# Linear-attention sums kv with the features as the loaded operand, in 32 by 32 outputs, without a transpose

## The chip, the core and the metric

The kernel runs on one core of a Trainium2 chip. The metric is the device time of one execution in microseconds (us). A core has five engines with instruction lists of their own: TensorE (PE in the profile; its weight loads are shown apart, as PEld), VectorE (DVE), ScalarE (ACT), GpSimd (POOL) and SyncE (SP, here the main DMA queue). TensorE multiplies a loaded operand (the stationary one, held in the 128x128 array) by a streamed one (the moving one) and writes to PSUM, which has banks of 128 partitions by 512 f32 values.

## The reference

Two branches read the same x (2048 rows, 512 columns) and are mixed by a gate. The change is in the first branch.

```python
# A: linear attention, 32 heads of 16
q, k, v = x @ wqkv                                    # split by head
pq = einsum("bhsd,hdf->bhsf", q, w_phi); pk = einsum("bhsd,hdf->bhsf", k, w_phi)
phi_q = concatenate([softmax(pq), softmax(-pq)])      # 32 features for each head
phi_k = concatenate([softmax(pk), softmax(-pk)])
kv  = einsum("bhsf,bhsd->bhfd", phi_k, v)             # sums over all 2048 rows: 32 x 16 for each head
z   = phi_k.sum(over s)
num = einsum("bhqf,bhfd->bhqd", phi_q, kv)
o   = num / (einsum("bhqf,bhf->bhq", phi_q, z) + 1e-6)
a   = o @ wo
# B: dense 512 -> 1376, Mish, 1376 -> 512
b   = mish(x @ w1 + b1) @ w2
g   = sigmoid(x . gate_w)
out = g * a + (1 - g) * b
```

## The kernel before

The kernel has two stages. Stage A goes over x in 8 chunks of 256 rows (two tiles of 128). It makes the features of k (a tile E of 128 rows by 1024 columns: two softmaxes of 512) and the values v (128 x 512), adds E up into zacc on POOL, adds E times v up in PSUM (kv), and stores the projected q to DRAM. Stage B goes over 4 blocks of 512 rows: the dense branch by 11 column tiles (up, then mi, hi, lo on ACT and POOL, then dn), the features of q, the product with kv (nu), the output projection (wo), and the mix. Large products are made of f32 split into a high and a low part in the rounded f32r type, three products for each; kv, num and the fused weights (fuse) are plain f32 products.

The order on every engine is written out by hand. Strings such as FIRST, EVEN, ODD, NEXT, LAST (stage A) and BLOCK0, BLOCK1, BLOCK (stage B) list steps by name; a word with a quote mark belongs to the chunk before, one with a plus to the next. The wrapper `pin` keeps each engine's instructions in the order in which they were written, and all matmuls go through the helper `mm` (line 101), all ACT work through `act` (line 121). So an engine that waits holds up everything behind it in its own list.

The steps that the change touches:

- `kv` (line 322) is run as `kv' kv` at the end of chunks 1, 3 and 5 (ODD), so for two chunks at once, and once for each of the chunks 6 and 7, in LAST. All sums go to one PSUM bank of the tag "kv", 256 of its 512 columns. For each of a chunk's two tiles it goes over u = 0..7 and r = 0, 1. One product loads 32 columns of v (two heads of 16) and streams 64 columns of E (the same two heads, both softmaxes, a = 0, 1). The output has 32 partitions (v) and 64 columns (features). Its start partition, 0, 32, 64 or 96, goes round with u and r.
- `km` (line 449, DVE) multiplies the sums by `mask`, which keeps the blocks in which feature and value belong to the same head, and writes them twice, spread over 512 columns.
- `kt_` (line 455, in BLOCK0 between up3 and mi3) turns this by four TensorE transposes of 128x128 against the identity `ident`, into a PSUM bank of the tag "a" (a ring of three that up, half of num, half of wo and the projections share), and ACT copies it to `kvb` (features in the partitions).
- `nu` (line 593) loads 64x32 pieces of kvb and streams the features of q, 256 columns, in all four blocks.
- `ident` and `mask` are made on POOL at the start (lines 188 to 192).

Of the kernel before, what the change touches and what calls it, by code (L numbers as in the profile page):

```python
# [8 lines left out]

F32 = mybir.dt.float32  # L10
# [5 lines left out]
P = 128  # L16
# [5 lines left out]
NG = 4  # L22
SC = 256
NCH = S // SC
# [36 lines left out]

BLOCK0 = """
    up0 mi0 hi0 lo0 gr lq3 S1 rS1 mx2 mn2 d02 d12 up1 @z mi1 hi1 lo1 T0 D0 m0 de0 rd0 sc0 es0 tr0 up2 mi2 hi2 lo2 dn0
    T1 D1 m1 de1 rd1 sc1 es1 tr1 mv0 lq0+ lq1+ mx3 mn3 d03 d13 up3 @kt mi3 hi3 lo3 dn1
    up4 mi4 hi4 lo4 WL0 dn2 E2 S2 T2 rS2 D2 m2 de2 rd2 sc2 es2 tr2 up5 mi5 hi5 lo5 WL1 dn3 E3 ge gg up6 mi6 hi6 lo6 dn4
    up7 mi7 hi7 lo7 dn5 nu0 oh0 S3 T3 rS3 ol0 D3 m3 de3 rd3 sc3 es3 tr3 mv1 up8 mi8 hi8 lo8 dn6
    mx0+ mn0+ d00+ d10+ mx1+ mn1+ d01+ d11+ lq2+ lq3+ wo0 ag0 wo1 ag1 E0+ E1+ S0+ T0+ rS0+ D0+ m0+ de0+ rd0+ sc0+ es0+ tr0+
# [22 lines left out]
def tile_gated_mix(ctx: ExitStack, tc: tile.TileContext, xT, wv, wkT, wqT, bd, w1a, w1b, b1, w2a, w2b, wo, out):  # L90
    nc = tc.nc
    const = ctx.enter_context(tc.tile_pool(name="const", bufs=1))
# [4 lines left out]
    pin = tc.keep_in_program_order  # L97
    V, G_, A_, Sy = nc.vector, nc.gpsimd, nc.scalar, nc.sync

    def mm(*a, **k):  # L100
        return pin(nc.tensor.matmul(*a, **k))  # L101

    def T(shape, dt, tag, bufs, name):
        nm[0] += 1
        return sp.tile(shape, dt, name=f"{name}_{nm[0]}", tag=tag, bufs=bufs)
# [7 lines left out]
    def k2(name, tag, dt=F32):  # L113
        return T([P, 512], dt, tag, {"pq": 3, "io": 4, "hl": 8}[tag], name)

    def psum(name, tag, bufs={"a": 3, "dn": 4, "kv": 1}):
        nm[0] += 1
        return pp.tile([P, 512], F32, name=f"{name}_{nm[0]}", tag=tag, bufs=bufs[tag])

    def act(out_, in_, fn=AF.Copy, **k):  # L120
        return pin(A_.activation(out_, in_, fn, **k))  # L121
# [60 lines left out]
    md = k2("md", "io")[:, :P].rearrange("p (h f) -> p h f", f=DH)  # L182
# [2 lines left out]
    pin(G_.affine_select(md, md, pattern=[[DH, 8], [0, DH]], compare_op=ALU.is_ge, fill=0.0, base=DH - 1, channel_multiplier=-1))  # L185
    b1s = const.tile([P, NF], F32, name="b1s")
    pin(G_.dma_start(b1s, b1))
    ident = const.tile([P, P], F32, name="ident")
    make_identity(nc, ident)
    mask = const.tile([P, 2, 2, 32], F32, name="mask")  # L190
    for a in range(2):
        pin(G_.tensor_add(mask[:, :, a, :], *[md[:, o : o + 4, :].rearrange("p (r h) f -> p r (h f)", r=2) for o in (0, 4)]))
    g_sb = const.tile([P, S // P], F32, name="g_sb")
    og_sb = const.tile([P, S // P], F32, name="og_sb")
    ge_sb = const.tile([P, S // P], F32, name="ge_sb")
    kvb = const.tile([P, NG, P], F32, name="kvb")


    steps = {}
# [1 line left out]
    def at(key, name, fn):  # L201
        steps.setdefault((key, name), []).append(fn)
# [11 lines left out]
    kvs = []  # L214
# [69 lines left out]
    def a_ops(c):  # L284
        key = ("A", c)
        P_ = psA[c] = {}
        for t in range(2):
            d = {}
            Es[c, t] = d

            def k_(t=t):
                P_["k", t] = proj(xs[c], t, wkh, wkl, "a")

            def v_(t=t):
                P_["v", t] = proj(xs[c], t, wvh, wvl, "dn" if c or t else "kv")

            def q_(t=t):
                P_["q", t] = proj(xs[c], t, wqh, wql, "a")

            def ve(t=t):  # L300
                vs[c, t] = k2("v", "io")
                act(vs[c, t], P_["v", t])

            def qe(t=t):
                P_["qs", t] = k2("qs", "pq")
                act(P_["qs", t], P_["q", t])

            def st(t=t):
                i = 2 * c + t
                pin(Sy.dma_start(pqd[i * P : (i + 1) * P, :], P_["qs", t]))  # L310

            at(key, f"k{t}", k_)
            at(key, f"v{t}", v_)
            at(key, f"q{t}", q_)
            at(key, f"ve{t}", ve)
            at(key, f"qe{t}", qe)
            at(key, f"st{t}", st)
            feat_ops(key, t, lambda t=t: P_["k", t][:, :], d)
            at(key, f"ml{t}", lambda d=d: scale_by(d, V))
            at(key, f"z{t}", lambda d=d: pin(G_.tensor_add(zacc, zacc, d["E"])))  # L320

        def kv():
            if not kvs:
                kvs.append(psum("kvp", "kv")[:, : NG * 64].rearrange("p (g f) -> p g f", g=NG))
            (kvp,) = kvs
            for t in range(2):
                E, v = Es[c, t]["E"], vs[c, t]
                Ev = E[:, :].rearrange("p (a r b x) -> p b r a x", a=2, r=2, b=8)
                for u in range(8):
                    for r in range(2):  # L330
                        o = (u % 2) * 64 + 32 * r
                        mm(kvp[o : o + 32, u // 2, :], v[:, u * 64 + 32 * r : u * 64 + 32 * r + 32], Ev[:, u, r, :, :],
                           start=(c == 0 and t == 0 and u < 2), stop=(c == NCH - 1 and t == 1), skip_group_check=True)

        at(key, "kv", kv)
        if c + 1 < NCH:
            def xh():
                new_x(c + 1)
                for j in range(2):
                    x_hi(c + 1, j)  # L340

            at(key, "xh", xh)
            for j in range(2):
                at(key, "xl", lambda j=j: x_lo(c + 1, j, G_))
        if c + 2 < NCH:
            at(key, "ldx", lambda: ldx(c + 2))
# [91 lines left out]
    B = {}  # L438

    def mid_ops():  # L440
        key = ("A", NCH - 1)

        def zh():
            B["zs"] = [k4("zs", "tx", F32R) for _ in range(2)]
            act(B["zs"][0], zacc)

        def km():
            B["km"] = k2("km", "io")
            shape = [P, NG, 2, 64]
            m = mask[:, :, :, :].rearrange("p r a f -> p r (a f)")[:, None, :, :].to_broadcast(shape)  # L450
            pin(V.tensor_mul(B["km"][:, :].rearrange("p (g r f) -> p g r f", g=NG, r=2), kvs[0][:, :, None, :].to_broadcast(shape), m))

        def kt_():
            pt = psum("kvT", "a")
            for G in range(NG):
                pin(nc.tensor.transpose(pt[:, G * P : (G + 1) * P], B["km"][:, G * P : (G + 1) * P], ident))  # L456
            act(kvb, pt[:, :].rearrange("p (g d) -> p g d", g=NG))

        def z():
            B["zb"] = k4("zb", "z")  # L460
            for a in range(2):
                ps = psum("z", "dn")
                for j in range(2):
                    mm(ps, onr, B["zs"][j][:, a * 512 : (a + 1) * 512], start=(j == 0), stop=(j == 1))
                act(B["zb"][:, a * 512 : (a + 1) * 512], ps)

        at(key, "zh", zh)
        at(key, "zl", lambda: pin(V.tensor_sub(B["zs"][1], zacc, f32(B["zs"][0]))))
        at(key, "km", km)
        at(("B", 0), "@kt", kt_)  # L470
        at(("B", 0), "@z", z)


    def b_ops(b):
        key = ("B", b)
        U, dn, tts, eTs, num, ohl, io = {}, {}, {}, {}, {}, {}, {}
# [66 lines left out]
        for t in range(4):  # L543
            d = {}
# [40 lines left out]
        for h in range(2):  # L585
            def mv(h=h):
                eTs[h] = k8("eT", "eT", F32)[:, :].rearrange("p (t q x) -> p t q x", t=2, q=4)
                for q in range(4):
                    for k in range(4):
                        o = 64 * (k % 2) + 32 * (k // 2)  # L590
                        pin(Sy.dma_start(eTs[h][o : o + 32, :, q, :], tts[h][32 * q : 32 * q + 32, :, k, :]))

            def nu(h=h):
                ev = eTs[h][:, :, :, :].rearrange("p t q (b c) -> p b (t q) c", c=32)
                po = [psum("num", tag) for tag in ("kv", "a")]
                for bh in range(2):
                    for c in range(4):
                        u = 4 * bh + c
                        for r in range(2):
                            o = (u % 2) * 64 + 32 * r  # L600
                            mm(po[r][32 * c : 32 * c + 32, bh * SC : (bh + 1) * SC], kvb[64 * r : 64 * r + 64, u // 2, o : o + 32], ev[64 * r : 64 * r + 64, u, :, :], start=True, stop=True, skip_group_check=True)
                for r in range(2):
                    num[h, r] = po[r]

            def oh(h=h):
                for gp in range(2):
                    ohl[h, gp] = k4("ohl", "oh", F32R)
                    act(ohl[h, gp][:, :512], num[h, gp])

            def ol(h=h):  # L610
                for gp in range(2):
                    pin(V.tensor_sub(ohl[h, gp][:, 512:], num[h, gp], f32(ohl[h, gp][:, :512])))  # L612

            at(key, f"mv{h}", mv)
            at(key, f"nu{h}", nu)
            at(key, f"oh{h}", oh)
            at(key, f"ol{h}", ol)
# [97 lines left out]
    for j in range(2):  # L715
        h, l = [w[:, 2 * j : 2 * j + 2, :].rearrange("p k f -> p (k f)") for w in (wvh, wvl)]
# [93 lines left out]
```

## Time and profile before

| what | value |
|---|---|
| median of 3 runs | 451.06 us (450.77 to 451.5) |
| profiled execution | 451.0 us, its span 449.3 us |
| granted TensorE clock, mean | 0.999 |
| PE busy | 443.9 us (99% of the span) |
| DVE, ACT, POOL busy | 306.0, 195.0, 163.0 us |
| TensorE time of kvp, by the chain | 1.7% of the span |

The profile shows one execution. The span runs from the first to the last instruction; the execution's own time is 1.7 us longer. The groups name a line, an engine, an operation and the tiles out<-in; for matmuls the line is that of the helper, 101, so they are told apart by tiles: kvp are the sums, kvT the transposes, num the product with kv. A matmul record lasts from its start to the modelled end of its passage through the array, so records overlap, and the sum of durations is more than the time taken. The chain of work that ended last is given in pieces: start, length, engine and group, number of instructions.

### The profile page before, as it was taken

Reading aid. Unit: us, or ns where it says so; the run is one execution under the profiler, and the core shown is the slowest. Engines: PE = TensorE matmul, PEld = TensorE weight load, DVE = VectorE, ACT = ScalarE, POOL = GpSimd, SP = SyncE. Lnnn points to the kernel's source line nnn. Section 1 sums busy time; section 2 is a strip of 40 time slices with the busy share of each in tenths; the row PEclk is TensorE's granted clock in tenths of the full one; section 3 lists DMA queues with packets and bytes.
Section 4 is the critical chain, followed back from the end, with each engine's and each line's share of the span. In section 5 each row is a group of like instructions: output and inputs, shape, how many; then the busy total and the mean of one; then the engine's idle time right before and its main releaser. Section 6 shows DMA issues by size and latency. Waiting matters only on the chain.

```text
span 449.3 us, 7222 instructions
## 1 busy us (share of the span) xinstructions
PE 443.9 (99%) x2886; PEld 362.8 (81%) x2886; DVE 306.0 (68%) x408; ACT 195.0 (43%) x269; POOL 163.0 (36%) x102
## 2 busy tenths in 40 slices
PE   8999999999999999999999999999999999999997
PEld 7888888888888888878787887887887888787885
DVE  2798558459399999997979976476967529611003
ACT  3644533444325555627355453534253543244221
POOL 3448687677862345621122212014212122221211
PEclk9999999999999999999999999999999999999999
DMA  7721522514523111405143151331151302030002
GB/s 272 268 95 47 190 69 95 190 15 172 189 84 106 48 24 25 117 19 154 64 125 111 39 148 48 82 107 47 36 149 47 86 13 95 1 82 13 1 0 95
DMA packets 25883, 40.09 MB, mean 89 GB/s; under 512 B 5749, under 2 KB 14197, under 8 KB 25849
## 3 DMA queue, kind: packets, MB, share of 16 engines
q1 hardware_dynamic: 25528, 39.22, 28.6%
q8 instruction: 23, 0.38, 0.3%
q10 hardware_dynamic: 288, 0.39, 0.3%
q14 instruction: 12, 0.09, 0.1%
q0 software_dynamic: 32, 0.01, 0.0%
HBM read 22.82 MB, written 8.40 MB: 69 GB/s over the span
## 4 chain that ended last, share of the span: by engine, by line
PE 98%; DMA 1%; ACT 0%; DVE 0%; issue 0%
PE proj L101 29%; PE up L101 27%; PE down L101 26%; PE wo L101 10%; PE num L101 2%; PE kvp L101 2%; DMA bds<-in_bd_dram 1%; PE fuse L101 1%; PE rest L101 0%; PE z L101 0%; ACT wkh L121 0%; PE warm L101 0%; DVE io L653 0%; PE kvT L456 0%
## 5 line engine op out<-in xcount | busy, mean ns | idle before, releaser
L500 POOL TENSOR_TENSOR l<-act,h 128x512 fp32r<-128x512 f32 x44 | 63.2, 1438 | 221.9 <-ACT h L121 183.6
L121 ACT ACTIVATE act<-up,b1s 128x512 f32<-128x512 f32 x44 | 30.3, 688 | 89.0 <-PE up L101 88.8
L320 POOL TENSOR_TENSOR zacc<-zacc,E 128x1024 f32<-128x1024 f32 x16 | 39.7, 2483 | 42.7 <-DVE E L282 32.6
L121 ACT ACTIVATE E<-E 128x1024 f32<-128x1024 f32 x32 | 33.6, 1059 | 47.3 <-DVE E L267 44.3
L282 DVE TENSOR_TENSOR E<-E,Sm 128x1024 f32<-128x1024 f32 x32 | 45.7, 1427 | 1.1
L271 DVE TENSOR_REDUCE Sm<-E 128x64 f32<-128x1024 f32 x32 | 38.7, 1210 | 5.0 <-ACT E L121 5.0
L101 PE MATMUL wo<-woh,ohl 128*128 128x512 f32 x128 | 40.7, 389 | 0.0
L101 PE MATMUL down<-w2ah,h 128*128 128x512 f32 x96 | 37.5, 390 | 0.0
L101 PE MATMUL down<-w2al,h 128*128 128x512 f32 x96 | 37.4, 390 | 0.0
L101 PE MATMUL down<-w2ah,l 128*128 128x512 f32 x96 | 37.4, 389 | 0.0
L258 DVE TENSOR_REDUCE mx<-proj 128x32 f32<-128x512 f32 x16 | 11.0, 690 | 30.7 <-PE proj L101 30.7
L101 PE MATMUL down<-w2bh,h 128*128 128x512 f32 x78 | 30.5, 391 | 0.0
L101 PE MATMUL down<-w2bl,h 128*128 128x512 f32 x78 | 30.4, 390 | 0.0
L101 PE MATMUL down<-w2bh,l 128*128 128x512 f32 x78 | 30.4, 389 | 0.0
L121 ACT ACT_TABLE_LOAD x19 | 24.4, 1283 | 10.1 <-PE up L101 9.8
L121 ACT ACTIVATE h<-act 128x512 fp32r<-128x512 f32 x44 | 27.8, 632 | 1.4
L612 DVE TENSOR_TENSOR ohl<-num,ohl 128x512 fp32r<-128x512 f32 x16 | 10.3, 683 | 26.5 <-ACT ohl L121 26.3
L101 PEld LDWEIGHTS wo<-woh,ohl 128*128 128x128 f32 x128 | 24.0, 188 | 5.0
L101 PE MATMUL up<-xbh,w1ah 128*128 128x512 f32 x96 | 26.2, 395 | 0.0
L101 PE MATMUL up<-xbh,w1al 128*128 128x512 f32 x96 | 25.7, 390 | 0.0
L101 PE MATMUL up<-xbl,w1ah 128*128 128x512 f32 x96 | 25.7, 390 | 0.0
L405 DVE TENSOR_TENSOR xbl<-xraw,xbh 128x1024 fp32r<-128x1024 f32 x8 | 12.2, 1562 | 19.8 <-ACT xbh L121 19.8
(121 smaller groups left out, 966.6 us busy)
## 6 DMA issues: line engine op xcount, KB each, us to landing
eT<-tt SPq DMA_DIRECT2D x128, 64.0 KB, 2.0
xraw<-in_xT_dram SPq DMA_DIRECT2D x15, 512.0 KB, 4.4
pqd<-qs SPq DMA_DIRECT2D x16, 256.0 KB, 3.1
pq<-pqd SPq DMA_DIRECT2D x16, 256.0 KB, 2.9
out_dram<-io SPq DMA_DIRECT2D x15, 256.0 KB, 2.1
raw<-in_w1a_dram SPq DMA_DIRECT2D x3, 512.0 KB, 4.3
raw<-in_w2a_dram SPq DMA_DIRECT2D x3, 512.0 KB, 4.0
wT<-in_wkT_dram SPq DMA_DIRECT2D x4, 256.0 KB, 5.2
```

Source lines behind the costliest of these rows:

```text
L101: return pin(nc.tensor.matmul(*a, **k))
L121: return pin(A_.activation(out_, in_, fn, **k))
L258: pin(V.tensor_reduce(d[name], hv(src()), axis=AX.X, op=op))
L271: pin(V.tensor_reduce(d["S"], hv(d["E"][:, :]), axis=AX.X, op=ALU.add))
L282: pin(eng.tensor_mul(hv(d["E"][:, :]), hv(d["E"][:, :]), d["S"][:, :, None].to_broadcast([P, 2 * H, DH])))
L320: at(key, f"z{t}", lambda d=d: pin(G_.tensor_add(zacc, zacc, d["E"])))
L405: pin(V.tensor_sub(xb[b][1][:, :, sl], kt(raw[h], SC), f32(xb[b][0][:, :, sl])))
L500: pin(G_.tensor_sub(U[i]["l"], U[i]["a"], f32(U[i]["h"])))
L612: pin(V.tensor_sub(ohl[h, gp][:, 512:], num[h, gp], f32(ohl[h, gp][:, :512])))
```

## The change

The operands of the sums change places: 32 columns of E (two heads, one softmax) are loaded and 32 columns of v are streamed, so there are two products, for a = 0 and 1, where there was one. The output has features in the partitions (start partition 64r + 32a) and values in the columns, which is the layout that `nu` loads. So the transposes, their PSUM bank, the copy to kvb and the identity go. `km` writes kvb directly, 256 columns in place of 512. The mask becomes 128x32, made by three dependent adds. `nu` reads kvb[:, u, :], in pieces of the same shape as before.

```diff
-    T1 D1 m1 de1 rd1 sc1 es1 tr1 mv0 lq0+ lq1+ mx3 mn3 d03 d13 up3 @kt mi3 hi3 lo3 dn1
+    T1 D1 m1 de1 rd1 sc1 es1 tr1 mv0 lq0+ lq1+ mx3 mn3 d03 d13 up3 mi3 hi3 lo3 dn1
...
-    ident = const.tile([P, P], F32, name="ident")
-    make_identity(nc, ident)
-    mask = const.tile([P, 2, 2, 32], F32, name="mask")
-    for a in range(2):
-        pin(G_.tensor_add(mask[:, :, a, :], *[md[:, o : o + 4, :].rearrange("p (r h) f -> p r (h f)", r=2) for o in (0, 4)]))
+    mask = const.tile([P, 32], F32, name="mask")
+    for o in (2, 4, 6):
+        pin(G_.tensor_add(mask, md[:, :2, :].rearrange("p h f -> p (h f)") if o == 2 else mask, md[:, o : o + 2, :].rearrange("p h f -> p (h f)")))
...
-    kvb = const.tile([P, NG, P], F32, name="kvb")
+    kvb = const.tile([P, 8, 32], F32, name="kvb")
...
-                kvs.append(psum("kvp", "kv")[:, : NG * 64].rearrange("p (g f) -> p g f", g=NG))
+                kvs.append(psum("kvp", "kv")[:, :256].rearrange("p (u d) -> p u d", u=8))
...
                 Ev = E[:, :].rearrange("p (a r b x) -> p b r a x", a=2, r=2, b=8)
                 for u in range(8):
                     for r in range(2):
-                        o = (u % 2) * 64 + 32 * r
-                        mm(kvp[o : o + 32, u // 2, :], v[:, u * 64 + 32 * r : u * 64 + 32 * r + 32], Ev[:, u, r, :, :],
-                           start=(c == 0 and t == 0 and u < 2), stop=(c == NCH - 1 and t == 1), skip_group_check=True)
+                        for a in range(2):
+                            o = 64 * r + 32 * a
+                            mm(kvp[o : o + 32, u, :], Ev[:, u, r, a, :], v[:, u * 64 + 32 * r : u * 64 + 32 * r + 32],
+                               start=(c == 0 and t == 0 and u == 0), stop=(c == NCH - 1 and t == 1), skip_group_check=True)
...
         def km():
-            B["km"] = k2("km", "io")
-            shape = [P, NG, 2, 64]
-            m = mask[:, :, :, :].rearrange("p r a f -> p r (a f)")[:, None, :, :].to_broadcast(shape)
-            pin(V.tensor_mul(B["km"][:, :].rearrange("p (g r f) -> p g r f", g=NG, r=2), kvs[0][:, :, None, :].to_broadcast(shape), m))
-
-        def kt_():
-            pt = psum("kvT", "a")
-            for G in range(NG):
-                pin(nc.tensor.transpose(pt[:, G * P : (G + 1) * P], B["km"][:, G * P : (G + 1) * P], ident))
-            act(kvb, pt[:, :].rearrange("p (g d) -> p g d", g=NG))
+            pin(V.tensor_mul(kvb, kvs[0], mask[:, None, :].to_broadcast([P, 8, 32])))
...
-        at(("B", 0), "@kt", kt_)
...
-                            o = (u % 2) * 64 + 32 * r
-                            mm(po[r][...], kvb[64 * r : 64 * r + 64, u // 2, o : o + 32], ev[64 * r : 64 * r + 64, u, :, :], start=True, stop=True, skip_group_check=True)
+                            mm(po[r][...], kvb[64 * r : 64 * r + 64, u, :], ev[64 * r : 64 * r + 64, u, :, :], start=True, stop=True, skip_group_check=True)
```

## The prediction

> **What bounds the kernel now.** I read the page first (engine shares, granted clock, chain by line), then the chain of waits in order of time, then the answers by tile for everything that the diff touches.
>
> ```profile
> PE 443.9 (99%) x2886; PEld 362.8 (81%) x2886; DVE 306.0 (68%) x408; ACT 195.0 (43%) x269; POOL 163.0 (36%) x102
> ...
> PEclk9999999999999999999999999999999999999999
> ...
> PE 98%; DMA 1%; ACT 0%; DVE 0%; issue 0%
> ```
>
> TensorE is the bound from the first product to the last, at full clock. It hardly waits for anybody, so only two things can move the time: the length of its own list of work, and a new wait on that list. Work taken from other engines is worth nothing here. In the chain by time:
>
> ```profile
> 15.36 2.02 PE fuse L101 x128
> ...
> 44.81 1.92 PE kvp L101 x128
> ...
> 138.29 1.03 PE kvp L101 x64
> ...
> 166.19 0.44 PE kvT L456 x4
> ```
>
> The sums of kv stand on the chain five times: three double runs of 1.92 us (44.8, 79.6, 114.4) and two single ones of 1.03 us (138.3, 150.4), 7.82 us together. The transposes stand on it once with 0.44 us. That is all of the chain that the diff edits; the product with kv (num) keeps its shapes.
>
> ```profile
> L101 PEld LDWEIGHTS kvp<-E,v x512: 106/110/111, 44.7 to 151.2; 128*32 128x32 f32 x171
> L101 PE MATMUL kvp<-E,v x512: 218/219/244, 44.7 to 151.2; 128*32 128x64 f32 x171
> L451 DVE TENSOR_TENSOR km<-kvp,mask x1: 627/627/627, 157.1 to 157.1; 128x512 f32<-128x512 f32 x1
> ```
>
> The code issues 8 chunks x 2 tiles x 16 = 256 products and the trace has 512 matmuls, so an f32 product is two instructions with a weight load each. Below, a pair is one load and one matmul.
>
> **How long a pair takes, and why.** A matmul record is 219 ns long, but a double run has 128 in 1.92 us, 15.0 ns each: several are in flight. The start times in the trace say how. In a run four matmuls start 6.7 ns apart (four outputs at partitions 0, 32, 64, 96), then nothing, and 56.0 ns after the first comes the next four. A double run is 32 such groups, 32 x 0.056 = 1.79 us, plus 0.13 us of turning from and to other work; a single one is 16 x 0.056 + 0.13 = 1.03. What are the 56 ns? The four transposes stream 128 columns each over the whole array and start 108 ns apart, the last warm-up products (128 f32 columns) 112 ns apart, some 0.83 ns a column; 64 columns are 53.3 ns. So one strip of the array is busy for 53.3 ns with its 64 columns, four strips work side by side, and 2.7 ns are overhead: the stage is bound by streaming, not by the number of instructions, as far as this trace goes.
>
> **The change part by part.**
>
> *kv sums.* 512 products, so 1024 pairs; each streams 32 columns of v in place of 64 of E, and loads 32 columns as before. The order of the outputs is again 0, 32, 64, 96, so four strips still work side by side. If streaming remains the bound, a group of four takes 32 x 0.83 = 26.7 ns plus overhead, and there are 256 groups in place of 128. For the overhead the trace has two rows. In kvp it is 2.7 ns, but there the load (32 columns) is half as long as the stream (64). After the change both are 32. The fuse stage has that ratio, 64 loaded and 64 streamed:
>
> ```profile
> L101 PEld LDWEIGHTS fuse<-bds,wT x256: 129/135/136, 6.0 to 17.1; 64*64 64x64 f32 x128
> L101 PE MATMUL fuse<-bds,wT x256: 218/218/268, 6.0 to 17.2; 64*64 64x64 f32 x128
> ```
>
> Loads of 32, 64 and 128 columns last 110, 135 and 188 ns (kvp, fuse, z), so loading costs 0.8 ns a column too, and a strip can't be ahead with its loads when they are as long as its stream. There the groups of four come 58.5 ns apart, 5.2 ns over the stream; it shows in the chain (128 matmuls in 2.02 us against 1.92). I take 26.7 + 5.2 = 31.9 ns, because the ratio is that of fuse: 256 x 0.0319 + 5 x 0.13 = 8.82 us, which is 1.00 us more than 7.82. With the overhead of kvp (29.4 ns) it is 8.18, 0.36 more. The other end: if a pair keeps its 15.0 ns however short its stream, 1024 pairs cost twice 7.82, 7.8 us more. A gain I exclude here: the columns streamed per strip are the same and the groups are twice as many. The row nearest to the new shape is fuse, so +1.00 stands in the sum.
>
> Four pairs at 6.7 ns are 26.7 ns, just under 31.9. That is the tight spot: the trace shows this rate only inside a group, never kept up over more than eight.
>
> The Trainium skill speaks against the change at this spot: TensorEngine Tiling, section Instruction Overhead, gives each matmul some 60 cycles, says a free dimension of 1 takes as long as one of 60, and advises not to tile a dimension that is already small. By that rule 32 columns would gain nothing over 64 and the sums would cost 7.8 us more; no stream in this trace is short enough to try it. The Trainium skill's page TensorE: Matmul & The Clock Gate (section Wait — 56ns, not 53.3ns?) has a floor of about 25 ns from start to start, which the trace's 15.0 ns a matmul contradicts across strips; along one strip no run here shows it.
>
> *Transposes.* Four matmuls and the turn to them go. From the start of the product before (165.80) to that of the second product after (166.70) pass 0.90 us, of which two ordinary steps of 0.227 are 0.45; 0.45 us go from the chain, in agreement with the 0.44 above.
>
> *Off the path.* ACT loses the eviction kvb<-kvT (0.60 us at 166.7). km on DVE writes 128x256 in place of 128x512: 0.63 becomes about 0.42 by the 128x256 row wkl<-fuse (0.41 to 0.43). It is still followed by the same reductions, and kvb is ready near 157.5, 33 us ahead of num at 191.1. TensorE waits for neither engine here, so 0. The bank that kvT took between up3 and up4 in the ring of three is now up4's; each user still gets the bank of three users before, so no new wait. POOL loses ident's memset and select (0.20 and 0.29) and has three dependent adds of 128x32 for two of 128x64 (0.33 each); its set-up ends at 4.3 us and its next work starts at 14.8, so 10 us cover that. No DMA is moved.
>
> *Inputs.* E becomes the loaded operand, v the streamed one. DVE has finished E before the runs begin (43.2 for 44.8, 77.9 for 79.6, 112.7 for 114.4, 147.4 for 150.4), so which operand is needed first costs 0.
>
> *Sum*, against the profiled execution, 451.0 us (span 449.3, 1.7 around it; the median of the runs, 451.06, is the same): +1.00 - 0.45 = +0.55, that is 451.6 us. With the small overhead -0.1.
>
> **Rivals.**
>
> *The number of pairs becomes the bound (slower).* TensorE can't take pairs faster than some rate above 8.0 ns (31.9 / 4), the point from which this decides. For it: no stretch of the trace sustains more than a pair in 14 ns. Against it: 6.7 ns inside groups of four and of eight (num). At 10 ns a pair the sums cost 1024 x 0.010 + 0.65 = 10.9 us, +3.1, and 453.6 us in all; at the 15.0 ns of today, 458.4 us. I give 0.35, one third of it to the full price, 458.4. The Trainium skill's rule in TensorEngine Tiling, cited above, would mean that full price.
>
> *Instruction blocks arrive late (slower).* TensorE's program comes in blocks:
>
> ```profile
> q8 instruction: 23, 0.38, 0.3%
> ```
>
> 0.38 MB for the page's 2 x 2886 = 5772 instructions are about 66 bytes each, and 0.38 MB / 23 is 16.5 KB, so some 250 to a block. A double run now uses up one block in 1.9 us and would use two. In the trace the third run (79.6 to 81.5) is followed by blocks at 83.4 and 87.0 only, some 1 us each. If few are held in store, each of the three double runs would stop for 1 to 2 us: 3 to 6 us on top of 451.6, 454.6 to 457.6 us. Against it: the 24 warm-up, 256 fuse and 48 projection pairs up to 17.4 us are 656 instructions, 2.6 blocks, one of them delivered by then, and nothing stalls, so at least two were in store. I give 0.1. The Trainium skill, in Runtime: NRT & Kernel Launch, section Instruction fetch mechanics, gives TensorE 128 KiB in one sentence and two lines of 16 KiB in another; by the first no stop comes, and no run here decides it.
>
> *A real gain.* The chain holds only 0.45 us to remove, so over 0.9 us needs something beyond it, a strip that streams 32 columns in less than half of 53.3 ns (20 ns a group of four would give 256 x 0.020 + 0.65 = 5.8 us, and 448.5 in all). Against it: 0.83 ns a column in every f32 row. 0.05.
>
> **Numbers.** The stream-bound forecast has 0.5, by itself 450.8 to 452.0. A measurement of this kernel tells 0.2% (0.9 us) from no change, so 450.2 to 452.0 is the same. Of the forecast 0.44 lie there, 0.05 above (an overhead of 7 ns would do), 0.01 below. Slower: 0.05 + 0.35 + 0.1 = 0.50; faster: 0.05 + 0.01 = 0.06. The range goes from 450.6 to 456.5: it leaves out the gain (0.06), the full price of the pair-bound rival (0.12) and the end of the late blocks (0.02), and takes in the rest.
>
> **What would show it.** In the changed profile: 1024 matmuls 128x32 in kvp, double runs of 256 at about 2.17 us, single ones of 128 at 1.15, no kvT, no new idle time of PE. A double run near 3.8 us proves the pair-bound rival. Pauses at one place within a run, different from run to run, with a block landing at their end, prove the blocks. If the kvp runs are as forecast and the time is not, the step that failed is the one that calls all else covered.

## The result, and the profile after

The changed kernel takes 463.03 us (median of 6 runs, 461.06 to 464.9), against 451.1 for the kernel before: ratio 1.0264, with a 95% interval of 1.0251 to 1.0277. The forecast of 451.6 us and the whole range (450.6 to 456.5) are missed. The profiled execution is the quickest of the six, 461.06 us with a span of 459.2 (449.3 before). Its page:

```profile
PE 447.8 (98%) x3394; PEld 365.9 (80%) x3394; DVE 305.6 (67%) x408; ACT 194.6 (42%) x268; POOL 162.9 (35%) x101
...
PEclk9999999899999999999999999999999999999999
...
q8 instruction: 26, 0.43, 0.4%
...
PE 97%; issue 2%; ACT 0%; DVE 0%
```

TensorE is still the bound, with 508 pairs more (512 for the sums, less 4 transposes). New are 2% "issue" in the chain, time in which the engine waited for nothing that the profile shows, and one slice with a lower clock. The chain in order of time (start, length, group) has the place:

```profile
44.50 1.79 PE kvp L100 x124
46.29 1.60 issue
47.89 0.92 PE kvp L100 x61
...
81.67 1.56 PE kvp L100 x113
83.23 5.01 issue
88.25 1.51 PE kvp L100 x95
89.75 33.51 PE proj L100 x144
123.26 2.46 PE kvp L100 x179
125.72 3.40 PE proj L100 x14
129.12 0.17 issue
```

TensorE stops in the middle of the first double run for 1.60 us, in the second for 5.01 us, and 3.4 us behind the third for 0.17 us; the third run itself goes through in 2.46 us. The two single runs follow at 148.19 and 160.56 with 1.25 and 1.30 us. (The numbers of instructions in this view leave some out: the timeline has 256 pairs in a double run, 179 of them ahead of the first stop and 161 ahead of the second.)

Where the 9.9 us of span went, by this chain: stops 1.60 + 5.01 + 0.17 = 6.78; the runs of sums without the stops 10.79 in place of 7.82, 2.97 more; the projections behind the second stop 33.51 in place of 32.86, and those behind the third run 3.40 + 18.90 in place of 21.98, together 0.97 more; from the first up product to the end 297.34 in place of 297.84, 0.50 less; the start 0.31 less. Sum 9.91. This is the quickest of the six executions. The spans of the others are 0.4 to 4.0 us longer, at mean clocks of 0.988 to 0.993 against 0.996 here, so the loss of clock that is described below is probably larger in them; their stops were not traced.

### The profile page after: what moved, and what is told of

It reads as the page before. It is cut to its first block, busy times and chain, and to the rows that moved or that the text cites. A ratio compares the mean times of both kernels' runs of the same rounds, so it can differ in the third digit from the quotient of the medians.

```text
span 459.2 us, 8235 instructions
## 1 busy us (share of the span) xinstructions
PE 447.8 (98%) x3394; PEld 365.9 (80%) x3394; DVE 305.6 (67%) x408; ACT 194.6 (42%) x268; POOL 162.9 (35%) x101
## 4 chain that ended last, share of the span: by engine, by line
PE 97%; issue 2%; ACT 0%; DVE 0%
PE proj L100 29%; PE up L100 26%; PE down L100 26%; PE wo L100 9%; PE kvp L100 2%; PE num L100 2%; PE warm L100 1%; PE fuse L100 1%; PE rest L100 0%; PE z L100 0%; ACT wkh L120 0%; DVE io L640 0%; DVE ones L169 0%
## 5 line engine op out<-in xcount | busy, mean ns | idle before, releaser
L279 DVE TENSOR_TENSOR E<-E,Sm 128x1024 f32<-128x1024 f32 x32 | 44.7, 1395 | 1.1
```

Source lines behind the costliest of these rows:

```text
L279: pin(eng.tensor_mul(hv(d["E"][:, :]), hv(d["E"][:, :]), d["S"][:, :, None].to_broadcast([P, 2 * H, DH])))
```

## The experiments

The theory after this result: TensorE's instructions come in blocks of 256, and a block is only fetched when an earlier one has been used up. A double run of 512 short instructions reaches the end of the block in hand before the next has come. I call it the block theory. The rivals: the pairs of the new shape are slow as such, E as the loaded operand is slow, or a run of some length fills something up.

**The runs apart.** In ODD, the sums of the chunk before are moved ahead, so that every run has 128 pairs:

```diff
-    k0 xh mx0 mn0 ...
+    k0 kv' xh mx0 mn0 ...
-    ... q1 qe1 st1 kv' kv
+    ... q1 qe1 st1 kv
```

> The changed kernel, with the sums of the chunk before moved from the end of the odd chunks to behind their first projection (k0): every run of sums has 128 pairs, with some 13 us of projections between two runs. Block theory (TensorE's next block of 256 instructions is asked for only when the one before it begins, and takes 3 to 6 us from then until it can run; a double run uses two blocks in 2.1 us): a run now needs one boundary at most, so the stops of 1.6 and 5.0 us fall under 0.5 us each; 8 runs of 1.25 to 1.30 us, 10.2 us in place of 7.8, less 0.45: 453.0 us. Rival, the pairs themselves are slow (each pair of this shape costs what it costs, stops included): the sums still cost 17 us or more and the time stays at 461 to 465 us.

Measured: 454.03 us, ratio 1.0065 (1.005 to 1.008). The chain has no stop in any run:

```profile
31.40 1.29 PE kvp L100 x99
...
46.56 1.40 PE kvp L100 x98
```

The other six are 1.25 to 1.29 us. So the same pairs, with the same operands, cost 9 us less when they stand apart; the time is still 0.65% above that of the kernel before. It is 1.0 us over what was expected. The runs are as priced (10.39 us together), but I left out that three more runs mean three more turns: besides the 0.13 us within a run, the projections behind each run take some 0.25 us over their steady step of 0.2267 us from start to start (13.83 to 13.87 us for 60 of them), 0.75 us together. The start was 0.2 us later too.

**The operands of before, streams cut in two.** The inner loop of the kernel before, with its transposes:

```diff
-  mm(kvp[o : o + 32, u // 2, :], v[:, ...32], Ev[:, u, r, :, :], ...)
+  for a in range(2):   # four strips in turn, then the other a
+      mm(kvp[o : o + 32, u // 2, 32 * a : 32 * a + 32], v[:, ...32], Ev[:, u, r, a, :], ...)
```

> The kernel before, with each stream of 64 columns of E cut into two of 32: v is still the loaded operand, the outputs keep their place and the transposes stay, but the pairs are 1024 as in the changed kernel, in the same runs. Block theory: the same instructions as in the changed kernel, so the same stops at the same places, first run after about 180 pairs, second after about 160; 463 us plus 0.45 for the transposes, 461.5 to 465.5 us. Rival, it is E as the loaded operand that is slow: no stops, double runs of about 2.2 to 2.5 us, 452 to 453 us.

Measured: 462.39 us (460.46 to 463.0), ratio 1.0235 (1.0211 to 1.0258).

```profile
44.77 1.74 PE kvp L101 x124
46.51 2.03 issue
...
82.32 1.56 PE kvp L101 x113
83.88 5.00 issue
```

The stops come after 179 and 161 pairs again, as in the changed kernel. For the stops it doesn't matter which operand is loaded; the number of pairs does.

**The same work, numbered otherwise.** The changed kernel, with 19 tiny products at the start, where TensorE waits for data:

```diff
     warm(WARM)
+    for j in range(19):
+        mm(pw[:32, :32], ones[:, :32], ones[:, :32], start=True, stop=True)
```

> The changed kernel with 19 tiny f32 products more (38 pairs, 76 instructions) behind the warm-up, where TensorE waits for data anyway. Nothing else is changed, but every later instruction has a number 76 higher. Block theory (boundaries at TensorE record 193 + 256 k): the first run starts at record 933 and has its block, so its stop goes, or is left after the run with under 1 us; the second run's stop moves from pair 161 to about pair 252 (record 2241) and stays at 3 to 6 us; the third run, which had none, stops at about pair 234 (record 3009) for 1.5 to 4 us. Time 460 to 466 us. Rival, the length of the run decides (something is full after some 160 to 180 pairs): the stops stay where they are, after 180 and 161 pairs, with 1.6 and 5.0 us, and the third run has none.

Measured: 466.19 us (two runs that agree within 0.03), ratio 1.0333 (1.0313 to 1.0354).

```profile
46.07 2.46 PE kvp L100 x179
...
51.70 1.42 issue
...
83.15 2.41 PE kvp L100 x176
85.56 4.53 issue
90.09 0.33 PE kvp L100 x4
...
125.56 2.33 PE kvp L100 x168
127.89 3.14 issue
131.03 0.40 PE kvp L100 x24
```

The first run is whole; its stop has moved behind it, into the projections (1.42 us, more than the 1 us I allowed, and the time is just above the 466 given). The second run stops after 250 pairs and the third, which had no stop, after 232, within two pairs of what was expected. No theory of shapes or of run lengths does that. The windows view counts matmuls and loads from the start up to each stop (PE busy and PEld busy, the number in brackets), first in the changed kernel:

```profile
0.00:46.29 46.29, 44.89 (x603) 37.51 (x604) 30.77 (x44) 22.99 (x39) 24.95 (x23) 1.00 0.49 166
0.00:83.22 83.22, 80.22 (x985) 66.79 (x985) 53.67 (x72) 36.98 (x58) 50.65 (x35) 1.00 0.44 142
0.00:129.10 129.10, 121.09 (x1494) 100.57 (x1494) 76.95 (x101) 52.76 (x79) 79.62 (x50) 0.99 0.41 132
```

and in the shifted one:

```profile
0.00:51.60 51.60, 50.20 (x731) 42.10 (x731) 31.00 (x45) 23.99 (x39) 28.71 (x26) 1.00 0.48 170
0.00:85.55 85.55, 82.72 (x1112) 68.98 (x1113) 53.80 (x72) 37.96 (x59) 51.55 (x36) 1.00 0.41 141
0.00:127.88 127.88, 120.53 (x1494) 100.04 (x1494) 76.69 (x100) 52.55 (x79) 76.17 (x47) 0.97 0.37 125
```

Sums of the two: 1207, 1970, 2988 and 1462, 2225, 2988. With TensorE's semaphore and drain instructions counted too, the stops come after 1217, 1985 and 3009 instructions in the changed kernel and after 1473, 2241 and 3009 in the shifted one. Each of these numbers is 193 plus a multiple of 256. The last stop of both has the same number, 2988, at different work (projections in the one, sums in the other).

The block's own records in the trace complete it. In the changed kernel the block for the first stop begins to move at 45.63 us, lands at 46.51, and TensorE goes on at 47.89, 1.38 us later; for the second 85.96, 86.89 and 88.25. In all runs with stops TensorE goes on 1.2 to 1.5 us after the landing.

The same records show when a block is fetched. Of the 26 blocks of the changed kernel and the 27 of the shifted one, none begins to move before TensorE has come within 42 instructions of the boundary one block ahead of its own first instruction. In the long products of the changed kernel from 185 us on, ten of eleven begin 28 to 42 instructions ahead of that boundary, and one begins 18 past it. This fits a store of two blocks, the one in use and the next. From the start of its move a block needs some 0.9 us to land and at least 1.2 us more until TensorE goes on, 2.1 us together. The 298 instructions (42 + 256) that TensorE has left by then take 1.4 us in an unbroken double run (2.46 us for 512); both sums are estimates from these records. So a run that crosses two boundaries, the first of them well inside it, has to stop at the second. The double runs of the two kernels bear this out: four stop, with the first boundary at instruction 67, 104, 210 or 247 of the run. In the two without a stop inside, it is at instruction 28 or 30, and the block for the second had begun to move 1.5 to 1.7 us ahead of the run.

**Traffic ahead of the block.** The changed kernel with two loads of 1 MB, used by nobody, ahead of the first double run:

```diff
+            if c == 1 and t == 0:
+                def extra():
+                    for _ in range(2):
+                        x = T([P, NFB * 512], F32, "w2b", 2, "extra")
+                        pin(A_.dma_start(x[:, :2048], w2b[:, :2048]))
+
+                at(key, "qe0", extra)
```

> The changed kernel, and ACT loads two times 1 MB that nobody uses, from 42.4 us on, 2 us ahead of the first double run, which had quiet queues. Block theory: the block that the first run waits for gets behind this traffic, so its stop grows from 1.6 us to 3.5 to 6 us, at the same pair (180); the time grows by about 2 to 4 us. Rival, a cost of the pairs or of the length of the run: the first run keeps its stop of 1.6 us.

Measured: 467.09 us, ratio 1.0353 (1.033 to 1.0376), 4.1 us more than the changed kernel's median.

```profile
46.31 4.47 issue
50.78 1.28 PE kvp L100 x76
```

The stop is after 179 pairs as ever, but 4.47 us long; its block begins to move at 48.51 us in place of 45.63. So traffic ahead of a block lengthens the stop. The two stops of the changed kernel differ in the same way: the block for the first begins to move 0.75 us after the boundary ahead of it was crossed, the block for the second 4.07 us after. That this is traffic too was not tried by taking the traffic away, but it fits. The traffic from 83.3 to 88.3 us, about the second, is:

```profile
q1 hardware_dynamic: 535, 1.41, 73.0%
q8 instruction: 1, 0.02, 1.2%
```

73% of the 16 engines' time, against 46.2% from 44.4 to 48 us, about the first. And a long stop costs more than its length. The windows of the changed kernel behind its second stop (granted clock in the third column from the end):

```profile
88.30:89.70 1.40, 1.40 (x96) 1.34 (x96) 0.00 (x0) 0.00 (x0) 0.00 (x0) 0.50 0.52 91
89.70:91.40 1.70, 1.70 (x8) 1.39 (x6) 0.00 (x0) 0.00 (x0) 0.00 (x0) 0.59 0.69 255
```

TensorE comes back at half its clock and has it back only some 2.8 us later; in the shifted kernel it stays at 0.50 for the whole of 90.1 to 95.0 us. All five stops of 4.47 to 5.01 us in these runs are followed by such a stretch, of 2.8 to 6.0 us of TensorE's work. Behind the stop of 1.60 us, one of 2.03 us with the streams cut in two, and one of 3.14 us in the shifted kernel, there is no such loss. The length of the stop alone does not tell when the clock falls: with the extra traffic it is 0.50 from 48.65 us on, 2.3 us after TensorE had stopped.

**What a pair costs.** The kernel with the runs apart, with half the columns in each load and stream. It leaves out the rest of the sums, and the product with kv uses ones:

```diff
-  mm(kvp[o : o + 32, u, :], Ev[:, u, r, a, :], v[:, ... + 32], ...)
+  mm(kvp[o : o + 16, u, :16], Ev[:, u, r, a, :16], v[:, ... + 16], ...)
```

> The kernel with the sums kept apart (every run 128 pairs, no stops), but each pair loads 16 columns of E and streams 16 of v; it leaves out the rest of the sums, and the product with kv uses ones. It measures what a pair costs when neither its load nor its stream can be the bound. If the loads and streams set the 32 to 33 ns of a group of four, groups fall to about 18.5 ns (13.3 and the 5.2 of overhead), or to 27 ns if the start of four pairs at 6.7 ns is next: a run falls from 1.29 to 0.75 or 1.0 us. If the supply of instructions sets it (about 8.3 ns a pair, as the regular spacing of 16.7 ns for two pairs in the middle of the runs suggests), the first 30 pairs or so go faster and the rest keep 8.3 ns: a run of 1.15 to 1.25 us. Time 452 to 454 us.

Measured: 452.98 us, ratio 1.0039 (1.0024 to 1.0053). Most runs take 1.19 to 1.20 us, where they took 1.29 with twice the columns:

```profile
67.14 1.19 PE kvp L100 x100
```

Half the work for each pair takes off 8% of a run. In the start times the first seven groups of four come every 25 ns; after that two pairs start every 16.7 ns, 8.33 ns a pair. With 32 columns it is 32 ns a group for the first eight groups and the same 16.7 ns for two pairs after that. So some 30 pairs start at a rate that depends on their columns, and after them a pair starts each 8.33 ns with 16 columns as with 32. I read this as a store of pairs that is worked off, and behind it the supply of instructions; the runs show that the columns don't set the 8.33 ns, not what does. The kernel before, with a pair each 14.0 ns, never felt this.

**The useful part alone.** The sums of the kernel before, and the transposes made on DVE in blocks of 32 by 32, with 8 DMAs that bring the blocks to the place where the changed kernel's km writes them:

```diff
+            pin(V.tensor_mul(B["km"].rearrange("p (u d) -> p u d", u=8), kvs[0]..., mask[:, None, :].to_broadcast([P, 8, 32])))
...
+            pin(V.transpose(t_, B["km"]))
...
+                        q, o = 64 * s + 32 * r, 64 * r + 32 * a
+                        pin(Sy.dma_start(kb[o : o + 32, s, :, :], tv[q : q + 32, a, :, :]))
```

> The sums of the kernel before (512 pairs, streams of 64), and only the transposes taken from TensorE: km writes 256 columns, DVE transposes them in blocks of 32 by 32 (0.4 us by its 128x1024 row of 1.25), and 8 small DMAs from SP, idle from 161 to 176 us, bring the blocks to the layout of the changed kernel's kvb, 25 us ahead of their first use. This is the part of the change that was to bring 0.45 us, alone. If that price is right: 0.3 to 0.5 us less than before, 450.6 to 450.8 us, ratio 0.999. Rival, the transposes were free (hidden behind the up and down products): the same time as before. Rival, the DMAs or the longer DVE list delay something that TensorE needs: over 451.5.

Measured: 452.25 us against 451.02, ratio 1.0018 (1.0004 to 1.0031): slower, the last rival. From the first up product (151.69) to the first num (190.93) it is 39.24 us in place of 39.70 before, so the 0.46 us are there. They are lost after that, in num and in the output projection wo:

```profile
190.93 1.47 PE num L100 x32
...
214.39 1.55 PE num L100 x32
...
218.91 5.74 PE wo L100 x24
```

In the kernel before each num takes 1.02 us and this wo 5.44 us. With 0.2 us at the start, the two num and the wo make the span 1.0 us longer (450.3 against 449.3) in spite of the 0.46 us. Only the first num was followed. The features of q reach num through DVE (E<-E,Sm, then the transpose) and 16 DMAs from SP, which began at 175.94 us before and at 179.55 us here. DVE was held up:

```profile
174.88 3.33 DVE L279 TENSOR_TENSOR E<-E,Sm 128x1024 f32<-128x1024 f32 x1
```

1.22 us before; it also began 1.5 us later (174.88 against 173.37). POOL's wol runs from 174.72 to 177.12 us here, and ran from 175.71 before, when DVE was past this step. Two places later in DVE's list were tried:

> As the kernel with the transposes on DVE, but the block transpose and the 8 DMAs stand behind the first transpose of the features of q (tr0, about 168 us), so the DVE list up to there is that of the kernel before, less 0.27 us. If the loss of that kernel came from the new meeting of DVE with POOL on its way to the features' transfers (DVE's E<-E,Sm took 3.33 us in place of 1.22 while POOL's wol ran, and the transfers began at 179.6 in place of 175.9 us), and this place meets POOL less, then num gets its data in time (1.02 us) and the time is 0.3 to 0.5 us under before: 450.5 to 450.8, ratio 0.999. Else 451.5 to 452.5 again.

> The same with the block transpose and the DMAs in front of the first T0 (about 162 us). Same expectations: with the transfers of the features starting by 177 us it gains 0.3 to 0.5 us, with a start near 179 us or later it loses about 1 us.

Measured: behind tr0 450.67 us, ratio 0.9995 (0.9985 to 1.0004); ahead of T0 450.51 us, ratio 0.9994 (0.9985 to 1.0003), both against 450.87. The transfers of the features begin at 175.12 and 174.49 us, E<-E,Sm takes 1.23 us, and num 1.02:

```profile
190.08 1.02 PE num L100 x32
```

From the first up product to the first num both take 39.25 us in place of 39.70, so the step's price is there. The medians of the time are 0.2 and 0.36 us lower, but both intervals hold 1: no version here is shown to beat the kernel before. Part of the reason lies outside the span. The spans are 448.2 to 449.2 us behind tr0 and 448.2 to 449.1 ahead of T0, against 449.0 to 449.8 before, so 0.3 and 0.5 us shorter in the median; the time around the span, 1.7 to 1.8 us in all executions before, reaches 2.5 and 2.9 us in some of these. Why it does was not found.

## Why the prediction was wrong

*Which case.* I gave 0.5 to the case in which streaming stays the bound, 0.35 to a bound by the number of pairs, 0.1 to late blocks. Both rivals came true together, and the late blocks make up most of the loss. The step that failed is the one that left waits for instruction blocks out of the sum. The sum has no term for them, and their rival got 0.1, because I concluded from a start without stalls that "at least two were in store" and took that to be comfort. In the profiled execution the stops are 6.78 of the 9.9 us. The count behind that conclusion was off too: the trace has 24 projection pairs up to 17.4 us and not 48, so 608 instructions, 2.4 blocks. Two in store is what the records show, but two are not enough for 512 instructions in some 2.5 us, since the run begins somewhere inside the first, and the next is fetched only when one is nearly used up. The evidence was in the trace of before: I had seen a block begin to move at 83.4 us, 2 us behind the run that ended at 81.5 us (the second run, not the third as I wrote). A block that comes 2 us late for a run of 1.9 us was a block not needed yet; I should have asked at which instruction it would be needed with the run twice as dense.

*The price of a late block.* I put 1 to 2 us on each double run. It was 1.60 and 5.01 us, and 0.17 us behind the third, and the run with extra loads shows that the wait grows with the traffic at that moment. There was also a term I didn't have at all, the half clock after a long stop. Behind the second stop the projections take 0.65 us more than before, and the broken run takes 0.61 us more than an unbroken one (1.56 + 1.51 against 2.46). Not all of the 0.61 is the clock, since the first broken run, at full clock, takes 0.25 us more too (1.79 + 0.92).

The Trainium skill, in Runtime: NRT & Kernel Launch, section Instruction fetch mechanics, gives blocks of 16 KiB and calls the cost of crossing such a boundary mostly hidden. The block length agrees with the stops, whose places are multiples of 256 instructions apart; that the crossing is hidden holds at 113 ns an instruction (projections), not at 4 to 5 ns.

*The pair.* The second step that failed is the size of the term for the sums, +1.00. The array's part was right: groups of four come every 32 ns against a forecast of 31.9, but only the first eight of them. (The rows behind that forecast give 0.84 to 0.88 ns a column, 108 and 112 ns for 128, and not 0.83; this moves the term by less than 0.4 us.) I called the next limit "the tight spot" and gave it 0.35 because 6.7 ns had been seen inside groups. It is 8.33 ns, just above the 8.0 from which it decides. An unbroken double run takes 2.46 us against a forecast of 2.17, a single one 1.25 to 1.30 against 1.15, so all five would be 2.1 us more than before rather than 1.00, without any stop. The Trainium skill's rule against tiling small dimensions (TensorEngine Tiling, section Instruction Overhead) had the direction right and the size wrong: going from 64 to 32 columns lowers the pair from 14.0 to 8.33 ns, where the rule gives no gain. Twice 8.33 is still more than 14.0, so the change loses.

*What held.* The transposes: 0.50 us from the first up product to the end in the changed kernel, 0.46 us when taken away alone, against 0.45. km takes 0.36 us against 0.42. Nothing in ACT, POOL or DVE came on the path in the changed kernel: num takes 1.02 us as before. The inputs of the sums were in time. "Pauses at one place within a run", "with a block landing at their end", was the sign that I named for the block rival, and it is what the profile shows, save that the place is fixed by the instruction's number and not "different from run to run".

*What stays open.* That traffic holds a block back is shown by the time at which it begins to move, not where it waits. What sets the 8.33 ns is inferred. The 1.2 to 1.5 us from landing to going on have no record in the trace. Why DVE's step grows to 3.33 us was seen beside POOL's subtraction, but it was not tried with that taken away.

## What to carry to other kernels

When a change makes TensorE's instructions smaller and more numerous, count instructions as well as columns: how many stand in one dense stretch, where in that stretch the next block of 256 begins, and what traffic the fetch of that block meets. Spread dense stretches out among long products: here each of the eight runs apart paid a turn of some 0.4 us, and none met a stop. A time that jumps by microseconds after a small shift of the code, with an idle TensorE and "issue" as its releaser, points to a late block; the block's record, which lands just ahead of the restart, settles it.

## What the runs showed of the hardware

- TensorE's short f32 pairs (a load and a matmul) start every 8.33 ns each behind the first 30 or so of a run, with 16 columns as with 32.
- TensorE stops at fixed instruction numbers, 193 plus a multiple of 256 here, when the next block has not come; it goes on 1.2 to 1.5 us after the block's landing, and the stops measured here reach from 0.17 to 5.01 us.
- A block of TensorE's instructions begins to move at the earliest 42 instructions ahead of the end of the block two before it (changed and shifted kernel, 53 blocks).
- After the five stops of 4.47 to 5.01 us TensorE works at a granted clock of 0.50 for 2.8 to 6.0 us; after stops of up to 3.14 us it does not.
- Every run of sums costs a turn of some 0.38 us (0.13 in the run, 0.25 in the projections behind it).
